# Attention and two expert layers on one core: the second layer's tiles ordered by token count, without a static remainder tile

## The chip, the cores and the metric

The kernel runs on one core of a Trainium2 chip. The metric is the device time of one execution in microseconds. Matmuls run on TensorE; VectorE, ScalarE and GpSimd (POOL) do the rest, and SyncE (SP) issues most transfers.

## What is computed

The output of a clustered attention gives 1536 rows of 512 numbers. Two layers of eight experts follow. In the first, rows with a positive skip score go through the expert of their largest logit. In the second every row goes through one expert, up to a capacity of 384 rows each:

```python
def _moe2_ref(x, w_gate, w1, w2, capacity):
    logits = x @ w_gate
    expert_idx = np.argmax(logits, axis=1)
    ...                                     # gate_w: softmax probability of that expert
    for i in range(N):                      # the first `capacity` rows of each expert are kept
        e = expert_idx[i]
        if counts[e] < capacity:
            disp[e, counts[e]] = x[i]
    ...
    h = np.maximum(np.einsum('ecd,edf->ecf', disp, w1), 0.0)
    y = np.einsum('ecf,efd->ecd', h, w2)    # D = 512, F = 1024
    ...                                     # out[i] = gate_w[i] * y[expert, position]
```

## The kernel before, in words

Attention is followed by `Moe.run`, in which every engine's order is the order of the code. A tile of tokens is a list of row numbers (`gi`), filled by a gather on POOL (`xg`), transposed on TensorE (`psxT`) and copied out by ScalarE; two products with weights `w1` and `w2` follow (L1 and L2), and an indirect output on POOL writes the rows (`fin2`, with `si` as the addresses and `g` as the gates). All outputs write the same tensor, one after the other.

The second layer has these tiles, in this order: 128 slots for rows of expert 0 that skip the first layer (`SU`, the last of the loop over `n1`), 128 slots for expert 0's other rows (`sS`), 256 slots in two parts of 128 for each of experts 1 to 7, and 128 slots for one remainder tile, whose expert is known only at run time (`rO`, `self.SO`). What is still left goes through a loop at the end (`overflow`) that runs as often as a count of remainder tiles says. The first two tiles multiply in plain fp32. The tiles of 256 split weights and activations into two fp32r halves (`wh`, `wl`; `xh`, `xl`; `hh`, `hl`) and use three matmuls for one: an L1 of 8 groups of 128 rows x 4 x 3 = 96 matmuls of 256 columns, and for each part of 128 slots an L2 of 24 matmuls of 512 columns. The remainder tile has a plain L1 and a split L2. PSUM for L1 comes from two buffers (`pL1`); one holds two groups, which ScalarE (`hh`, relu) and VectorE (`hl`) read.

Weights come in eight pieces of 512 KB for each expert, into two alternating sets of buffers. The halves of piece 0 of the next tile are made after the first pair of groups of a tile, pieces 1 to 4 after its L1, and 5 to 7 after its L2 (`nsplit`: first `wh` on ScalarE, then `wl` on VectorE).

Which row goes to which slot is computed with one-hot matrices. `prefix` counts rows before a row on TensorE, `rank` reads the result, `make_R` builds twelve 128 x 128 one-hot matrices `R` on VectorE, and `spread` multiplies them with the columns to be moved. These steps are Python generators (`route2`, `route2b`, `ovinfo`), and `at(t, k, ...)` says before which matmul step of which tile the next piece of them is recorded. `T` is the tile `sS`, and `n1` the tile `SU`; `T, 4` is the fifth of the eight L1 steps of `sS`.

Of the kernel before, what the change touches and what calls it, by code (L numbers as in the profile page):

```python
# [459 lines left out]
class Moe:  # L460
    def __init__(self, ctx, tc, xa, xb, out, w1a, w2a, w1b, w2b, wg2, ident, landA, J=12):
# [44 lines left out]
        nc.gpsimd.iota(self.thr[2][:, 0, :], pattern=[[128, self.nov]], base=128, channel_multiplier=0,  # L506
                       allow_small_or_imprecise_dtypes=True)
# [11 lines left out]
        self.names = con.tile([128, E], F32, name="names")  # L519
        self.ovi = con.tile([128, 1], F32, name="ovi")  # L520
# [366 lines left out]
    def route2(self):  # L887
        V, sm, E, J = self.nc.vector, self.sm, self.E, self.J
        ohp = self.ohp[2]
        V.tensor_tensor(out=ohp, in0=self.acco, in1=self.cm, op=ALU.subtract)  # L890
        T = self.totals(ohp, J, "b", sm)
        yield
        ps = self.prefix(ohp, T, J)
        r = self.r[2]
        self.rank(ohp, ps, J, "b", sm, r)
# [7 lines left out]
        Mf = M.rearrange("p j e s -> p j (e s)")  # L903
        rhs = sm.tile([128, J, 2 * E, 2], BF16, name="rhs2", bufs=1)
        V.tensor_tensor(out=rhs, in0=Mf.unsqueeze(3).to_broadcast([128, J, 2 * E, 2]),
                        in1=self.cols2.unsqueeze(2).to_broadcast([128, J, 2 * E, 2]), op=ALU.mult)
        R = sm.tile([128, J, 128], BF16, name="R", bufs=1)
        self.make_R(R, rp, 0, J)
        yield
        p1 = self.spread(R, rhs, J)  # L910
        inf, t, S = self.ids(p1, 2 * E, sm, "f")
        self.S2 = S
        self.T2 = T
        self.st2 = (R, Mf, inf, t)
        yield

    def route2b(self, cap):
        V, sm, E, J = self.nc.vector, self.sm, self.E, self.J
        R, Mf, inf, t = self.st2
        S = self.S2  # L920
# [4 lines left out]
        self.dests(inf, t, 2 * E, S, sm, "f")  # L925
# [8 lines left out]
        rhs = sm.tile([128, J, 2 * E, 3], BF16, name="rhs5", bufs=1)  # L934
        V.tensor_tensor(out=rhs, in0=Mf.unsqueeze(3).to_broadcast([128, J, 2 * E, 3]),
                        in1=g3.unsqueeze(2).to_broadcast([128, J, 2 * E, 3]), op=ALU.mult)
        yield
        p2 = self.spread(R, rhs, J)
        self.rest(p2, 2 * E, S, sm, "f", 3)
# [119 lines left out]
    def l2(self, hh, hl, W2, rng, ps, sub=0):  # L1059
        nc = self.nc  # L1060
        cs = slice(sub * 128, sub * 128 + 128)
# [33 lines left out]
    def fin2(self, s, ps):  # L1095
        nc, sm = self.nc, self.sm
        y = sm.tile([128, self.D], F32, tag="xy", name="y2")
        nc.scalar.activation(out=y, in_=ps, func=AF.Copy, scale=s["g"])  # L1098
        nc.gpsimd.indirect_dma_start(out=self.out, out_offset=bass.IndirectOffsetOnAxis(ap=s["si"], axis=0),  # L1099
                                     in_=y, in_offset=None, bounds_check=N_TOK - 1, oob_is_err=False)  # L1100
# [131 lines left out]
    def dyn_cum(self, m, idx):  # L1232
# [7 lines left out]
        if m == 1:  # L1240
            V.scalar_tensor_tensor(out=e, in0=self.tix[:, 0:E], scalar=es, in1=self.names, op0=ALU.is_equal, op1=ALU.mult)
            V.tensor_reduce(out=es, in_=e, axis=AX.X, op=ALU.add)
# [53 lines left out]
    def run(self, lg, cap):  # L1296
        nc, E = self.nc, self.E
        n1 = E + 2
        N = n1 + E + 1
# [4 lines left out]
        def load(n, i, t=None):  # L1304
            if n >= N:
                return
            if n == N - 1:
                w = self.load(2, self.rO, n, i, t)
            elif n < n1:
# [3 lines left out]
            else:  # L1313
                w = self.load(2, n - n1, n, i, t)
# [5 lines left out]
        rL = {}  # L1320
# [23 lines left out]
        r1, r1c, r2, r2b = self.route1(lg), self.route1c(), self.route2(), self.route2b(cap)  # L1344
        W2 = lambda t: [L[t, i] for i in range(4, 8)]
        X = {}
        sub = lambda t: [self.S2[2 * t], self.S2[2 * t + 1]]
        PS = {}

        def alloc_x(t):  # L1350
            X[t] = [self.big.tile([128, 4, 256], F32R, name=n) for n in ("xh", "xl")]

        def xts(t, i):
# [4 lines left out]
            sl = slice(i * 128, i * 128 + 128)  # L1358
# [3 lines left out]
        def l1(t, k, hh, hl):  # L1362
            ps = self.pL1.tile([128, 2, 256], F32, tag="l1", name="psl1")
            xh, xl = X[t]
            for q in range(2):
                f = 2 * k + q
                for c in range(4):
                    wh, wl = SP[n1 + t, c]
                    fs = slice(f * 128, f * 128 + 128)
                    nc.tensor.matmul(ps[:, q, :], wh[:, fs], xh[:, c, :], start=(c == 0), stop=False)  # L1370
                    nc.tensor.matmul(ps[:, q, :], wh[:, fs], xl[:, c, :], start=False, stop=False)  # L1371
                    nc.tensor.matmul(ps[:, q, :], wl[:, fs], xh[:, c, :], start=False, stop=(c == 3))  # L1372
            sl = slice(2 * k, 2 * k + 2)
            nc.scalar.activation(out=hh[:, sl, :], in_=ps, func=AF.Relu)
            nc.vector.scalar_tensor_tensor(out=hl[:, sl, :], in0=ps, scalar=0.0, in1=hh.bitcast(F32)[:, sl, :],  # L1375
                                           op0=ALU.max, op1=ALU.subtract)

# [9 lines left out]
        def put2():  # L1387
            self.gather(2, self.S2[0])
# [48 lines left out]
        at(n1, 10, nx(r2), put2, nx(r2b))  # L1437
# [20 lines left out]
        sS = self.S2[0]  # L1458
# [6 lines left out]
        at(T, 0, nx(r2b))  # L1465
        at(T, 3, nx(r2b))
# [9 lines left out]
        ov = self.ovinfo(2)  # L1476
        self.count(2, self.T2)
        eO = self.dyn_cum(2, 0)
        for t in range(1, E + 1):
            n = n1 + t  # L1480

            def nsplit(*ii):
                for i in ii:
                    if n + 1 < N and (t + 1 < E or i >= 4):
                        split(n + 1, i)

            if t == E - 2:
                self.rO = self.reg(eO)
            if n + 2 < N:
                for i in range(4, 8):  # L1490
                    load(n + 2, i)
            hh, hl = self.new_h(256)
            if t < E:
                nxt = sub(t + 1) if t + 1 < E else self.SO[0:1]
                for s in nxt:
                    self.gather(2, s)
                for k in range(4):
                    l1(t, k, hh, hl)
                    if k == 0:
                        nsplit(0)  # L1500
            else:
                nxt = []
                for k in range(2):
                    self.l1_native(self.SO[0]["xt"], [L[n, i] for i in range(4)], k, hh[:, :, 0:128], hl[:, :, 0:128])
# [5 lines left out]
            for i, s in enumerate(sub(t) if t < E else self.SO[0:1]):  # L1510
                ps = self.ps2()
                W2 = [SP[n, j] for j in range(4, 8)]
                self.l2(hh, hl, W2, range(0, 4), ps, i)
                if i == 1 and t + 1 < E:
                    xts(t + 1, 1)
                self.l2(hh, hl, W2, range(4, 8), ps, i)
                self.fin2(s, ps)
                if i == 0 and t + 1 < E:
                    xts(t + 1, 0)
                elif t < E and i == 0:  # L1520
                    self.xt_native(self.SO[0])
            nsplit(5, 6, 7)
        self.overflow(2, [L[N - 1, i] for i in range(8)], 1)
# [92 lines left out]
```

## Time and profile before

| | |
|---|---|
| median of three runs | 669.7 us (669.12 to 671.2) |
| the profiled execution's own time | 668.53 us |
| its span on the core | 666.7 us |
| TensorE busy | 634.2 us, 95% |
| VectorE, ScalarE, GpSimd busy | 63%, 57%, 40% |
| HBM traffic over the span | 152 GB/s |

The span is what the profile shows of the core, from its first to its last instruction; the time holds about 2 us more. Matmuls are pipelined, so the busy time of one is longer than its pace.

### The profile page before, as it was taken

To read this page: it belongs to the slowest core of one execution; us is meant where nothing else is said; L and a number is where in the kernel's file an instruction comes from. 1 tells how busy PE (TensorE), PEld (TensorE's weight loads), DVE (VectorE), ACT (ScalarE), POOL (GpSimd) and SP (SyncE) were. 2 spreads that over 40 slices of the span, in tenths; PEclk is the share of its full clock that TensorE was granted. 3 is DMA by queue.
4 is the path that set the end of the run, shared out by engine and by line. 5 is a ranking of instruction groups with operands and counts; after the bars stand their busy time and mean duration, and the time that the engine had idled before them with its cause. 6 is when DMAs were issued, how large, how long until landed. Compare 5 with 4: busy or idle time off the path is not lost. (4 is left out here: it accounts for less than half of the span.)

```text
span 666.7 us, 11852 instructions
## 1 busy us (share of the span) xinstructions
PE 634.2 (95%) x4238; PEld 547.3 (82%) x4238; DVE 418.1 (63%) x1027; ACT 379.9 (57%) x626; POOL 263.4 (40%) x194
## 2 busy tenths in 40 slices
PE   7889999999998999999999999999999999999994
PEld 6768888888877788887798888986799889888984
DVE  5958666666778774334967766636854955646421
ACT  5767787878777779851443444312544546446340
POOL 7666676767666688800211111101022312302210
PEclk8999999999999999999999999999999999999998
DMA  8964838484834469421677888861596477367100
GB/s 234 210 129 116 204 82 202 82 195 92 205 65 92 119 165 371 124 80 52 186 279 277 313 314 314 328 242 48 187 374 233 166 262 257 129 230 260 36 32 3
DMA packets 78960, 121.49 MB, mean 182 GB/s; under 512 B 27569, under 2 KB 42929, under 8 KB 78896
## 3 DMA queue, kind: packets, MB, share of 16 engines
q1 hardware_dynamic: 74416, 108.18, 53.4%
q0 software_dynamic: 4480, 12.50, 5.7%
q8 instruction: 35, 0.57, 0.4%
q14 instruction: 29, 0.24, 0.1%
HBM read 87.90 MB, written 13.37 MB: 152 GB/s over the span
## 5 line engine op out<-in xcount | busy, mean ns | idle before, releaser
L301 POOL TENSOR_TENSOR Pl<-P,Ph 128x768 fp32r<-128x768 f32 x93 | 170.4, 1841 | 67.7 <-ACT Ph L299 33.4
L983 DVE TENSOR_TENSOR wl<-l,wh 128x1024 fp32r<-128x1024 f32 x92 | 109.2, 1220 | 51.5 <-ACT wh L982 51.0
L272 DVE TENSOR_REDUCE m<-psx 128x1 f32<-128x384 f32 x192 | 97.9, 549 | 33.3 <-PE psx L271 32.1
L290 PE MATMUL pss<-BB,AA 128*128 128x384 f32 (+1 forms) x384 | 88.2, 352 | 9.4 <-DVE lg L372 3.6
L298 ACT ACTIVATE P<-pss 128x384 f32<-128x384 f32 x192 | 84.0, 489 | 21.8 <-PE pss L290 17.0
L982 ACT CAST wh<-l 128x1024 fp32r<-128x1024 f32 x92 | 92.5, 1048 | 0.0
L299 ACT CAST Ph<-P 128x768 fp32r<-128x768 f32 x96 | 80.1, 835 | 4.3 <-PE pso L318 1.2
L290 PEld LDWEIGHTS pss<-BB,AA 128*128 128x128 f32 (+1 forms) x384 | 65.5, 190 | 16.0 <-ACT P L298 4.1
L1005 PE MATMUL psl<-xt,l 128*128 128x128 f32 x640 | 78.0, 277 | 0.4 <-ACT xt L1153 0.4
L1005 PEld LDWEIGHTS psl<-xt,l 128*128 128x128 f32 x640 | 74.9, 192 | 1.7 <-ACT xt L1153 0.5
L1099 POOL DMA_INDIRECT out_dram<-y,fsi x15 | 15.8, 1055 | 130.8 <-ACT y L1098 123.4
L316 PE MATMUL pso<-Ph,VA 128*65 128x384 f32 x192 | 65.5, 341 | 0.7 <-ACT DN L333 0.7
L318 PE MATMUL pso<-Ph,VL 128*64 128x384 f32 x192 | 65.7, 342 | 0.0
L320 PE MATMUL pso<-Pl,VA 128*65 128x384 f32 x192 | 65.3, 340 | 0.2 <-DVE Pl L301 0.2
L1370 PE MATMUL psl<-xh,wh 128*128 128x256 f32 x224 | 62.5, 279 | 2.5 <-DVE hl L1375 2.5
L1371 PE MATMUL psl<-xl,wh 128*128 128x256 f32 x224 | 62.0, 277 | 0.7 <-DVE xl L1360 0.7
L1372 PE MATMUL psl<-xh,wl 128*128 128x256 f32 x224 | 61.9, 276 | 0.0
L271 PE MATMUL psx<-AA,BB 128*128 128x384 f32 x192 | 51.6, 352 | 3.8 <-DVE m L272 1.4
L1091 POOL DMA_INDIRECT xb<-x,fsi x8 | 8.1, 1014 | 102.6 <-DVE x L1090 88.1
L1065 PE MATMUL psl<-wh,hh 128*128 128x512 f32 x120 | 48.2, 402 | 0.0
L1067 PE MATMUL psl<-wl,hh 128*128 128x512 f32 x120 | 47.2, 393 | 0.0
L1066 PE MATMUL psl<-wh,hl 128*128 128x512 f32 x120 | 46.8, 390 | 0.0
(403 smaller groups left out, 1186.9 us busy)
## 6 DMA issues: line engine op xcount, KB each, us to landing
l<-in_moe_w_dram SPq DMA_DIRECT2D x136, 512.0 KB, 7.1
AA<-qkH SPq DMA_DIRECT2D x14, 384.0 KB, 4.8
vn<-in_v_dram SPq DMA_DIRECT2D x8, 384.0 KB, 4.9
BB<-qkL SPq DMA_DIRECT2D x16, 192.0 KB, 3.1
xa<-xn SPq DMA_DIRECT2D x8, 384.0 KB, 3.1
xb<-xn SPq DMA_DIRECT2D x8, 384.0 KB, 4.1
AA<-qkL SPq DMA_DIRECT2D x31, 96.0 KB, 3.8
BB<-qkH SPq DMA_DIRECT2D x31, 96.0 KB, 3.0
```

Source lines behind the costliest of these rows:

```text
L272: nc.vector.tensor_reduce(out=hs[h]["m2"][:, qc, f:f + 1], in_=ps, axis=AX.X, op=ALU.max)
L290: nc.tensor.matmul(ps, AA[0:K, t, kc * 128:(kc + 1) * 128], BB[0:K, t, sl], start=(t == 0), stop=(t == 1))
L298: nc.scalar.activation(out=P[:, f * HF:(f + 1) * HF], in_=ps, func=AF.Exp, scale=1.0 / 8.0)
L299: nc.scalar.copy(Ph, P)
L301: eng.tensor_tensor(out=Pl, in0=P, in1=Ph.bitcast(F32), op=ALU.subtract)
L316: nc.tensor.matmul(o[0:D + 1, :], va, Ph[:, sl], start=(kc == 0), stop=False)
L318: nc.tensor.matmul(o[0:D, :], vl, Ph[:, sl], start=False, stop=False)
L320: nc.tensor.matmul(o[0:D + 1, :], va, Pl[:, sl], start=False, stop=(kc == C - 1))
L982: nc.scalar.copy(h, src)
L983: nc.vector.tensor_tensor(out=l, in0=src, in1=h.bitcast(F32), op=ALU.subtract)
L1005: nc.tensor.matmul(st[k][:, q, :], L1[c][:, f * 128:(f + 1) * 128], xt[:, c, :], start=(c == 0), stop=(c == 3))
L1370: nc.tensor.matmul(ps[:, q, :], wh[:, fs], xh[:, c, :], start=(c == 0), stop=False)
```

## The change

Experts 2 to 7 of the second layer are sorted by their counts at run time (`sort2`), and place `p` of the order, not expert `p`, owns a tile. The tiles have fixed sizes, `caps` = 128, 256, 320, 256, 256, 256, 256, 128; places 0 and 1 stay with experts 0 and 1. Weight addresses of places 2 to 7 are read from `namei2` into a register. A tile of 320 has three parts (128, 128, 64), one PSUM group at a time, and a piece of `h` of its own (`h3`). The remainder tile and its `ovinfo` step are gone from the straight part of the program, and the loop now starts at the first remainder tile. The routing is made in two rounds: `route2` finds the slots of experts 0 and 1, `sort2` those of the sorted order.

```diff
+        self.caps = [128, 256, 320] + [256] * (E - 4) + [128]
+        self.slots = [(p, i) for i in range(3) for p in range(E) if self.caps[p] > 128 * i]
...
+        self.kb = iota([128, E], [[-1, E]], E, 0, "kb")
+        for dst, base in [(self.thr[2][:, p, :], w) for p, w in enumerate(self.caps) if w != self.c0[2]] + \
+                [(self.kb[:, 0:1], 2 ** 18), (self.kb[:, 1:2], 2 ** 17)]:
+            nc.gpsimd.iota(dst, pattern=[[128, dst.shape[1]]], base=base, channel_multiplier=0,
+                           allow_small_or_imprecise_dtypes=True)
...
     def route2(self):
...
-        M = sm.tile([128, J, E, 2], BF16, name="M2", bufs=1)
-        V.tensor_tensor(out=M[:, :, :, 1], in0=ohp, in1=self.bc(s, E), op=ALU.mult)
-        V.tensor_tensor(out=M[:, :, :, 0], in0=ohp, in1=M[:, :, :, 1], op=ALU.subtract)
...
+        cnt = self.ps()[:, 0:E]
+        for b in range(2):
+            self.nc.tensor.matmul(cnt, self.ones, T[:, b], start=(b == 0), stop=(b == 1))
...
+        V.scalar_tensor_tensor(out=self.key2, in0=cnt, scalar=16.0, in1=self.kb, op0=ALU.mult, op1=ALU.add)
...
+    def sort2(self):
...
+        V.tensor_tensor(out=c, in0=key.unsqueeze(1).to_broadcast(G), in1=key.unsqueeze(2).to_broadcast(G), op=ALU.is_ge)
+        V.tensor_reduce(out=pos, in_=c, axis=AX.X, op=ALU.add)
+        V.tensor_tensor(out=c, in0=pos.unsqueeze(1).to_broadcast(G), in1=one.unsqueeze(2).to_broadcast(G), op=ALU.is_equal)
+        V.tensor_tensor(out=c, in0=c, in1=self.tix[:, 0:E].unsqueeze(1).to_broadcast(G), op=ALU.mult)
+        V.tensor_reduce(out=self.names2, in_=c, axis=AX.X, op=ALU.add)
+        V.tensor_copy(self.namei2, self.names2)
+        V.tensor_tensor(out=tv, in0=self.ohx, in1=pos.unsqueeze(1).to_broadcast([128, J, E]), op=ALU.mult)
+        V.tensor_reduce(out=pv, in_=tv, axis=AX.X, op=ALU.add)
+        ohp = self.ohp[2]
+        V.tensor_tensor(out=ohp, in0=self.bc(pv, E), in1=one.unsqueeze(1).to_broadcast([128, J, E]), op=ALU.is_equal)
+        yield
...
+        V.tensor_tensor(out=rhs, in0=M.unsqueeze(3).to_broadcast([128, J, K, 2]),
+                        in1=self.cols2.unsqueeze(2).to_broadcast([128, J, K, 2]), op=ALU.mult)
+        yield
+        inf, t, S = self.ids(self.spread(self.R2, rhs, J), K, sm, "v")
...
+        self.T2 = self.totals(ohp, J, "v", sm)
         yield
...
     def run(self, lg, cap):
...
-        N = n1 + E + 1
+        N = n1 + E
...
+            if n >= n1:
+                p = n - n1
+                if p > 1 and p not in r2n:
+                    r2n[p] = self.reg(self.namei2[:, p:p + 1])
+                w = self.load(2, r2n.get(p, p), n, i, t)
...
         def l1(t, k, hh, hl):
-            ps = self.pL1.tile([128, 2, 256], F32, tag="l1", name="psl1")
...
+            W = self.caps[t]
+            Q = 2 if W <= 256 else 1
+            for f0 in range(2 * k, 2 * k + 2, Q):
+                ps = self.pL1.tile([128, Q, W], F32, tag="l1", name="psl1")
...
+                for (h, l), a, b in [((hh, hl), 0, min(W, 256))] + ([(self.h3, 256, W)] if W > 256 else []):
+                    nc.scalar.activation(out=h[:, sl, 0:b - a], in_=ps[:, :, a:b], func=AF.Relu)
+                    nc.vector.scalar_tensor_tensor(out=l[:, sl, 0:b - a], in0=ps[:, :, a:b], scalar=0.0,
+                                                   in1=h.bitcast(F32)[:, sl, 0:b - a], op0=ALU.max, op1=ALU.subtract)
...
-        at(n1, 10, nx(r2), put2, nx(r2b))
+        at(n1, 10, nx(r2), put2, nx(rs))
+        at(n1, 13, nx(rs))
+        at(n1, 14, nx(r2b))
...
-        at(T, 0, nx(r2b))
-        at(T, 3, nx(r2b))
+        at(T, 0, nx(rs))
+        at(T, 1, nx(r2b))
+        at(T, 4, nx(r2b))
...
-        ov = self.ovinfo(2)
         self.count(2, self.T2)
-        eO = self.dyn_cum(2, 0)
-        for t in range(1, E + 1):
+        Z = E - 1
+        for t in range(1, E):
...
-            if 2 <= t <= 4:
-                next(ov)
...
-        self.overflow(2, [L[N - 1, i] for i in range(8)], 1)
+        self.overflow(2, [L[N - 1, i] for i in range(8)])
```

The first place where rows move is VectorE where the first layer hands over to the second. Before, the slots of all experts come in one round; `finf`, `ft` and `fgi` are the row numbers read from PSUM, `Ff`, `pT` and `urk` belong to the true ranks, `fsi` are output addresses:

```order
L648 COPY finf<-psq 128x32
L649 SCALAR_TENSOR_TENSOR ft<-finf 128x16
L650 TENSOR_SCALAR fgi<-ft 128x16
L923 CAST Ff<-acco 128x96
L604 TENSOR_REDUCE pT<-Ff 128x16
L657 TENSOR_SCALAR fz<-finf 128x16
L658 SCALAR_TENSOR_TENSOR fsi<-ft,fz 128x16
L1143 TENSOR_TENSOR accg<-accg,psq 128x36
L625 TENSOR_TENSOR urk<-Ff,psq 128x96
```

In the changed kernel the same place holds the sort and the masks of the sorted order (`ohx` is the one-hot matrix by expert, `ohp` the one by place), before the true ranks begin:

```order
L660 TENSOR_SCALAR fgi<-ft 128x4
L941 TENSOR_TENSOR rktt<-key_138 128x64
L942 TENSOR_REDUCE skp<-rktt 128x8
L943 TENSOR_TENSOR rktt<-skp,tix 128x64
L944 TENSOR_TENSOR rktt<-rktt,tix 128x64
L945 TENSOR_REDUCE names_136<-rktt 128x8
L946 CAST namei_137<-names_136 128x8
L947 TENSOR_TENSOR uval<-ohx,skp 128x96
L948 TENSOR_REDUCE skv<-uval 128x12
L950 TENSOR_TENSOR ohp_126<-skv,tix 128x96
...
L961 TENSOR_TENSOR rhs_6267<-M_6263,cols_119 128x360
```

Nine operations of the sort, three masks and a product stand between `fgi` and `Ff`; `urk` comes another six rows later.

The second place is VectorE at the start of the second tile of the loop (expert 2 before, place 2 after). Before, the last three weight halves (`wl`) of the tile ahead are followed by one `hl` of 512 columns for each pair of groups:

```order
L1360 TENSOR_TENSOR xl<-psxT,xh 128x4x128 x2
L983 TENSOR_TENSOR wl<-l_1_6441,wh 128x1024
L983 TENSOR_TENSOR wl<-l_2_6443,wh 128x1024
L983 TENSOR_TENSOR wl<-l_3_6445,wh 128x1024
L1375 SCALAR_TENSOR_TENSOR hl<-psl_6731,hh 128x512
L983 TENSOR_TENSOR wl<-l_0_6617,wh 128x1024
L1375 SCALAR_TENSOR_TENSOR hl<-psl_6762,hh 128x512
```

After, the three halves stand at the same place, and two pieces follow for each single group, the second of them into `hA` (the piece `h3`):

```order
L1420 TENSOR_TENSOR xl<-psxT,xh 128x4x64
L1037 TENSOR_TENSOR wl<-l_1_6509,wh 128x1024
L1037 TENSOR_TENSOR wl<-l_2_6511,wh 128x1024
L1037 TENSOR_TENSOR wl<-l_3_6513,wh 128x1024
L1438 SCALAR_TENSOR_TENSOR hl<-psl_6824,hh 128x256
L1438 SCALAR_TENSOR_TENSOR hA<-psl_6824,hA 128x64
L1438 SCALAR_TENSOR_TENSOR hl<-psl_6841,hh 128x256
L1438 SCALAR_TENSOR_TENSOR hA<-psl_6841,hA 128x64
L1037 TENSOR_TENSOR wl<-l_0_6692,wh 128x1024
```

One buffer of PSUM is free after two rows where one row freed it before, and holds half as many groups.

## Rows read from the trace of the kernel before

**Rows 1.** Busy time in stretches of the second layer: stretch, length, engines, PEclk, DMA share.

```profile
core 0: us, PE busy (x) PEld busy (x) DVE busy (x) ACT busy (x) POOL busy (x), PEclk, DMA share, GB/s
480.76:491.73 10.97, 10.97 (x100) 10.97 (x98) 5.87 (x15) 3.42 (x5) 3.19 (x3) 1.00 1.04 393
491.73:497.22 5.49, 5.49 (x27) 4.46 (x25) 4.41 (x5) 4.38 (x5) 0.00 (x0) 1.00 1.03 400
497.22:497.57 0.35, 0.35 (x5) 0.35 (x4) 0.35 (x1) 0.15 (x1) 0.00 (x0) 1.00 0.97 386
503.62:515.23 11.61, 11.17 (x97) 10.96 (x96) 6.52 (x7) 6.16 (x8) 4.47 (x3) 1.00 0.63 217
562.48:563.14 0.66, 0.66 (x27) 0.66 (x25) 0.00 (x0) 0.46 (x1) 0.00 (x0) 1.00 1.01 394
598.90:622.40 23.50, 23.06 (x154) 20.78 (x153) 13.22 (x14) 12.29 (x16) 5.15 (x4) 1.00 0.54 196
645.44:658.27 12.83, 12.82 (x89) 11.46 (x87) 4.79 (x5) 4.71 (x6) 0.99 (x1) 1.00 0.06 22
```

**Rows 2.** Timeline of TensorE, waits in brackets: start, us, instruction.

```profile
509.69 0.38 PE L1370 MATMUL psl<-xh,wh 128*128 128x256 f32 x1 [0.44 <-DVE hl L1375]
...
528.09 0.39 PE L1371 MATMUL psl<-xl,wh 128*128 128x256 f32 x1 [0.70 <-DVE xl L1360]
```

**Rows 3.** DMA page of the stretch with the last output alone, 658 to 663.

```profile
DMA packets 80, 0.02 MB, mean 4 GB/s; under 512 B 75, under 2 KB 75, under 8 KB 80
```

**Rows 4.** Costliest groups of the whole span: busy, mean ns of one.

```profile
L290 PE MATMUL pss<-BB,AA 128*128 128x384 f32 (+1 forms) x384 | 88.2, 352 | 9.4 <-DVE lg L372 3.6
...
L318 PE MATMUL pso<-Ph,VL 128*64 128x384 f32 x192 | 65.7, 342 | 0.0
```

**Rows 5.** Timeline of VectorE in the loop's second tile.

```profile
505.53 3.50 DVE L983 TENSOR_TENSOR wl<-l,wh 128x1024 fp32r<-128x1024 f32 x3 [3.17 <-ACT wh L982]
508.94 0.68 DVE L1375 SCALAR_TENSOR_TENSOR hl<-psl,hh 128x512 fp32r<-128x512 f32 x1
...
524.80 2.04 DVE L630 TENSOR_SCALAR R<-iob,oslF 128x128 bf16<-128x128 bf16 x12
```

**Rows 6.** Busy time in two stretches, early and after the last matmul.

```profile
12.61:16.02 3.41, 3.09 (x16) 2.31 (x17) 1.85 (x5) 2.80 (x4) 2.12 (x5) 0.50 1.02 224
...
661.00:661.50 0.50, 0.00 (x0) 0.00 (x0) 0.00 (x0) 0.00 (x0) 0.00 (x0) 0.64 0.06 17
```

**Rows 7.** Timeline of TensorE in the native tile sS.

```profile
464.09 0.19 PE L615 MATMUL psq<-pT,U 128*128 128x48 bf16 x1
...
464.99 2.94 PE L1005 MATMUL psl<-xt,l 128*128 128x128 f32 x24 [0.42 <-ACT xt L1153]
...
472.17 0.45 PE L640 MATMUL psq<-rhsU,R 128*128 128x3 bf16 x12
...
473.84 7.03 PE L1071 MATMUL psl<-l,hh 128*128 128x512 f32 x16
```

**Rows 8.** Timeline of VectorE at the handover.

```profile
453.81 0.25 DVE L626 TENSOR_REDUCE r<-brk 128x12 f32<-128x96 f32 x1
...
459.32 0.17 DVE L650 TENSOR_SCALAR fgi<-ft 128x16 int32<-128x16 f32 x1
...
469.16 2.03 DVE L630 TENSOR_SCALAR R<-iob,rU 128x128 bf16<-128x128 bf16 x12
```

**Rows 9.** Timelines of POOL: its first DMA, an output and a gather.

```profile
9.13 0.86 POOL L250 DMA_DIRECT2D AA<-qkH  x1 [1.66 <-DVE qkH L159]
...
475.32 1.02 POOL L1099 DMA_INDIRECT out_dram<-y,csi  x1 [11.37 <-ACT y L1098]
...
485.01 1.03 POOL L950 DMA_INDIRECT xg<-xb,fgi  x1 [0.30 <-issue]
```

**Rows 10.** DMA issues of the whole span: KB each, median us to landing.

```profile
l<-in_moe_w_dram SPq DMA_DIRECT2D x136, 512.0 KB, 7.1
...
xg<-xb,fgi POOLq DMA_INDIRECT x15, 5.1
...
out_dram<-y,csi POOLq DMA_INDIRECT x1, 7.6
```

More of the change, by code (lines that the diff above doesn't have):

```diff
@@ L909, in route2 @@
         yield
[L910 to L914, printed above, removed]
+        inf, t, S = self.ids(self.spread(R, rhs, J), 4, sm, "f")
+        self.S2 = {(0, 0): S[0], (1, 0): S[2], (1, 1): S[3]}
+        self.R2 = R
+        yield
+    def sort2(self):
+        V, sm, E, J = self.nc.vector, self.sm, self.E, self.J
+        G = [128, E, E]
+        one = self.tix[:, 1:E + 1]
+        c = sm.tile(G, F32, name="rktt", bufs=1)
+        pos = sm.tile([128, E], F32, name="skp", bufs=1)
+        pv = sm.tile([128, J], F32, name="skv", bufs=1)
+        tv = sm.tile([128, J, E], F32, name="uval", bufs=1)
+        key = self.key2
+        V.tensor_tensor(out=c, in0=key.unsqueeze(1).to_broadcast(G), in1=key.unsqueeze(2).to_broadcast(G), op=ALU.is_ge)
[9 more added lines that the diff above has]
+        yield
+        K, o = len(self.slots), 0
+        M = sm.tile([128, J, K], BF16, name="M2", bufs=1)
+        for i in range(3):
+            ps = [p for p, j in self.slots if j == i]
+            n = len(ps)
+            V.tensor_tensor(out=M[:, :, o:o + n], in0=ohp[:, :, ps[0]:ps[0] + n], in1=self.bc(self.smk[:, :, i], n), op=ALU.mult)
+            o += n
+        self.M2 = M
+        rhs = sm.tile([128, J, K, 2], BF16, name="rhs2", bufs=1)
+        V.tensor_tensor(out=rhs, in0=M.unsqueeze(3).to_broadcast([128, J, K, 2]),
+                        in1=self.cols2.unsqueeze(2).to_broadcast([128, J, K, 2]), op=ALU.mult)
+        yield
+        inf, t, S = self.ids(self.spread(self.R2, rhs, J), K, sm, "v")
+        for k, d in self.S2.items():
+            S[self.slots.index(k)] = d
+        self.dests(inf, t, K, S, sm, "v")
+        self.S2 = dict(zip(self.slots, S))
+        self.P2 = S
+        self.T2 = self.totals(ohp, J, "v", sm)
@@ L933, in route2b @@
         V.tensor_copy(self.cols5[:, :, 2:5], g3)
-        rhs = sm.tile([128, J, 2 * E, 3], BF16, name="rhs5", bufs=1)
-        V.tensor_tensor(out=rhs, in0=Mf.unsqueeze(3).to_broadcast([128, J, 2 * E, 3]),
-                        in1=g3.unsqueeze(2).to_broadcast([128, J, 2 * E, 3]), op=ALU.mult)
+        K = len(self.slots)
+        rhs = sm.tile([128, J, K, 3], BF16, name="rhs5", bufs=1)
+        V.tensor_tensor(out=rhs, in0=self.M2.unsqueeze(3).to_broadcast([128, J, K, 3]),
+                        in1=g3.unsqueeze(2).to_broadcast([128, J, K, 3]), op=ALU.mult)
         yield
-        p2 = self.spread(R, rhs, J)
-        self.rest(p2, 2 * E, S, sm, "f", 3)
+        p2 = self.spread(self.R2, rhs, J)
+        self.rest(p2, K, self.P2, sm, "v", 3)
         rhsU = sm.tile([128, J, 3], BF16, name="rhsU3", bufs=1)
@@ L1457, in run @@
         psU = ps
-        sS = self.S2[0]
+        sS = self.S2[0, 0]
         self.xt_native(sS)
@@ L1475, in run @@
         self.fin2(sS, psS)
-        ov = self.ovinfo(2)
         self.count(2, self.T2)
-        eO = self.dyn_cum(2, 0)
-        for t in range(1, E + 1):
+        Z = E - 1
+        for t in range(1, E):
             n = n1 + t
+            for i in range(4, 8):
+                load(n + 2, i)
             def nsplit(*ii):
                 for i in ii:
-                    if n + 1 < N and (t + 1 < E or i >= 4):
+                    if t + 1 < Z or t + 1 == Z and i >= 4:
                         split(n + 1, i)
[L1487 to L1491, printed above, removed]
-            hh, hl = self.new_h(256)
[L1493 to L1497, printed above, removed]
-                    l1(t, k, hh, hl)
[L1499 to L1504, printed above, removed]
@@ new lines, in run @@
+            hh, hl = self.new_h(256)
+            if self.caps[t] > 256:
+                h3 = self.rt.tile([128, 2, 8, 64], F32R, name="hA")
+                self.h3 = h3[:, 0], h3[:, 1]
+            nxt = sub(t + 1) if t < Z else []
+            for s in nxt:
+                self.gather(2, s)
+            for k in range(4 if t < Z else 2):
+                if t < Z:
+                    l1(t, k, hh, hl)
+                else:
+                    self.l1_native(sub(t)[0]["xt"], [L[n, i] for i in range(4)], k, hh[:, :, 0:128], hl[:, :, 0:128])
+                if k == 0:
+                    nsplit(0)
@@ L1505, in run @@
             nsplit(1, 2, 3, 4)
-            if 2 <= t <= 4:
-                next(ov)
             for i in range(4):
                 load(n + 2, i)
-            for i, s in enumerate(sub(t) if t < E else self.SO[0:1]):
+            pre = [lambda i=i: xts(t + 1, i) for i in range(len(nxt))] if t + 1 < Z else \
+                [lambda: self.xt_native(nxt[0])] if nxt else []
+            for i, s in enumerate(sub(t)):
                 ps = self.ps2()
+                w = width(t, i)
                 W2 = [SP[n, j] for j in range(4, 8)]
[L1513 to L1521, printed above, removed]
+                self.l2(hh, hl, W2, range(0, 4), ps, i, w)
+                if pre and (i or len(pre) == 3):
+                    pre.pop(0)()
+                self.l2(hh, hl, W2, range(4, 8), ps, i, w)
+                self.fin2(s, ps, w)
+                if pre and i == 0:
+                    pre.pop(0)()
```

95 lines of the change are left out of this document (49 added, 46 removed).

## Prediction

> **What bounds the kernel now.** I read the second layer tile by tile, first in the windows of single stages, then in the waits of TensorE, then in the other engines' timelines at the places where TensorE waits.
>
> In [rows 1] the reader is to see that from 480.76 us on TensorE is the bound and little else. The first product of expert 1's tile fills 10.97 us of 10.97, one second product of 128 slots 5.49 of 5.49, a whole later 256-slot tile is 23.06 busy of 23.50, and the remainder tile 12.82 of 12.83, all at a granted clock of 1.00 (2.4 GHz). VectorE (13.22) and ScalarE (12.29) have half of the 23.50 free, and the DMA engines are at 0.54. So a tile costs its matmuls times their pace: 10.97 / 96 = 114 ns for 256 columns, 5.49 / 24 = 229 ns for 512. The little that TensorE waits is in [rows 2]: 0.44 us at the third PSUM pair of the second tile, until VectorE has written `hl`, and 0.70 in the third tile, until VectorE has written `xl`.
>
> How full the slots are is not in the diff, but in the inputs. The reference on its drawn inputs gives experts 0 to 7 counts of 164, 147, 248, 244, 125, 186, 156 and 266, and the native tile of 128 takes 81 of expert 0's first. Hence only expert 7 passes 256, by ten tokens. The trace agrees: the remainder tile's output moved 0.02 MB [rows 3], ten rows of 2 KB.
>
> **The tiles.** In the new order the lists are 83, 147, 266, 248, 244, 186, 156, 125, and they fit 128, 256, 320, 256, 256, 256, 256, 128 with nothing left over, so the loop for the remainder has no pass. The last static tile has the form of the old remainder tile (native first product, split second) and costs the same 12.83. What goes is one 256-slot tile: -23.50 [rows 1].
>
> **The tile of 320.** Its first product is still 96 matmuls, now of 320 columns. Between 114 and 229 ns that is 114.3 + 64/256 x 114.5 = 143 ns: 13.72 us, +2.75. Its third part holds 64 slots, but takes 24 matmuls of 512 columns like a full one. Whether half a stationary operand is cheaper, [rows 4] tell: 64 columns by 384 take 342 ns, 128 columns by 384 take 352. So +5.49; the bound below, were time to follow the slots, is 2.75. The third part's transposes add 0.35 [rows 1].
>
> **A wait that grows.** The 320-wide PSUM tile holds one 128-row group instead of two, so each of the two buffers lasts 1.72 us of matmuls instead of 2.74. At the second tile's start (503.62) VectorE still has three weight splits from the tile before: they start at 505.53, when ScalarE gives the first half, and `hl` is begun at 508.94 [rows 5]. The order of the change keeps those splits ahead of the first `hl`. TensorE runs dry after two groups, 3.43 us after the start. The first group's buffer comes free after two `hl` pieces (256 and 64 columns; from 0.68 for 512 I estimate 0.35 and 0.2) plus 0.07, at 5.9 us. So it stands idle 2.47 us where it lost 11.61 - 10.97 = 0.64 before: +1.83. Bounds: 0 if the splits come earlier, 3.2 if VectorE takes as long for each piece as for 512 columns. Later groups need about 1.1 us of evacuation per 1.72 us of matmuls and don't wait.
>
> In that idle stretch the clock matters. After the last matmul of the kernel, at 658.27, the granted clock is still at full level until about 661 [rows 6], 2.7 us later, so a gap of 2.47 should pass at 2.4 GHz, with little to spare. The Trainium skill (TensorE: Matmul & The Clock Gate, section "Why this matters for your kernels") advises against idle gaps between bursts of matmuls, since the clock returns to its lower level; by that rule this stretch, not the tile count, would be the place to look. The trace has no such gap in the second layer; rival 2 prices it.
>
> **What the static remainder cost elsewhere.** Its slot numbers were computed on VectorE in tiles 2 to 4 and spread on TensorE in 0.66 us [rows 1]; the first part, whose last step runs from 524.80 to 526.84 on VectorE [rows 5], made `xl` late by 0.70 [rows 2]. Both go: -1.36.
>
> **The handover to the second layer.** The route is now made in two rounds: first for experts 0 and 1, then the sort, then all slots. Row by row: VectorE gets five more small operations before `R`, drops one mask, and saves as much again with masks of 48 and 96 columns instead of 96 and 384. The sort's nine operations follow `fgi` (459.32) at about 0.25 to 0.3 each (the reduce of 96 columns is 0.25 [rows 8]): 2.5 us, then masks and their product, 1.4: ready at about 463.5, before TensorE gets there at 464.09 [rows 7]. So the second spread finds its operand, and its 0.3 us lies in the time up to 464.99 in which TensorE waits for `xt`. The true-rank prefix, which lay in that time, comes one step of 0.93 later and costs about 0.45 on the path (464.09 to 464.99 less the 0.42 of waiting). With it the operand `rhs5` and all that VectorE does behind it move by about 1.9 us; `R` for the native tile, done at 471.19 [rows 8], ends at 473.1, and TensorE, which wants it at 472.17 + 0.45 [rows 7], waits 0.5. Together +0.9; bounds 0.4 (the wait is absorbed) and 2.4 (the whole shift appears).
>
> Behind that, the output of the native tile slips by 2 us. On POOL it starts at 475.32 and lands 7.6 later [rows 9, 10]; the next output, which writes the same tensor, waits for that, and the gathers behind it start at 485.01. They would start at 487 and land by 494.6 even at those 7.6; the first one is needed after expert 1's first product and half a second one, at 480.76 + 0.9 + 10.97 + 2.75 = 495.4. Nothing is added, but the margin is under a microsecond.
>
> **At nothing.** Weight addresses come from registers: tile 2's name is ready near 461, and its first load waits for a buffer that TensorE frees at 473.84 [rows 7]. Five more IOTAs at the start run in the 1.66 us in which POOL waits before its first DMA [rows 9]; uncovered they would cost well under 1. A ninth expert's weights are no longer loaded, 4 MB in a stage that doesn't wait for DMA.
>
> **Sum.** -23.50 + 2.75 + 5.49 + 0.35 + 1.83 - 1.36 + 0.90 = -13.54. From the profiled execution's 668.53 that is 655.0. The median of the three runs is 669.7, 1.2 above it, which gives 656.2. I take the middle, 655.6.
>
> **The rivals.**
> 1. No new stall in the 320 tile: VectorE gets its `hl` in early. For it: VectorE is half idle there. Against: the order puts the splits first. -1.83 and the old 0.64 gone: 653.1.
> 2. The gap lowers TensorE's clock. For it: the margin of [rows 6] is small. The stretch at 1.2 GHz that the trace has, early in attention, is 3.41 us long [rows 6]; at half pace that loses 1.7: 657.3.
> 3. The handover costs its upper bound, or the first gather is late: +1.5 to +2, 657.3.
> 4. The other side: a list is too long and the loop for the remainder makes a pass. It decides when the shortest list passes 128 (it has 125), the longest 320 (266) or the next 256 (248). A pass is in series: 12.83 for the products, 4 MB of weights at about 395 GB/s [rows 1] 10.6, a gather of 5.1 [rows 10], 28.5 together even without its output: 684, slower by 14. The counts speak against it, and the ten rows of [rows 3] bear them out.
> 5. The change doesn't give what it says, since loads by register come late: each late weight tile costs up to its 7.1 us [rows 10]. One such wait leaves -6.4: 662.7. Against it: the first layer loads by register too.
>
> **How the numbers follow.** The sum has 0.70 (654 to 657 by its small bounds), rival 1 0.07, rivals 2 and 3 0.08 each, rival 5 0.04, rival 4 0.03. The time is that of the sum. The range goes from rival 1 to rivals 2 and 3 with half a microsecond on the slow side: 653.0 to 658.3. A measurement of this kernel can tell about 0.3%, 2 us; all cases but rival 4 are faster by more: 0.96, with 0.01 for no difference and 0.03 for slower.
>
> **What would show it.** Right: the second tile lasts about 33.6 us instead of 23.50, with one wait near 2.5 us at its third group, on `hA` or `hl`; no matmul of the output `ogi`; five tiles of 256 in place of seven, each near 23.5; TensorE ends near 644.7 at clock 1.00. The spread of 30 columns starts without a wait. Wrong: a wait for `xg` in expert 1's tile, a wait for weights `l`, PEclk under 1.00 after the gap, or a pass of the loop behind the last tile.

## The result, and the profile after

The changed kernel takes 659.83 us in the median of six runs (658.66 to 660.74); the kernel before took 670.11 beside it. The ratio is 0.9845, with a 95% interval of 0.983 to 0.986. The gain is 10.3 us where 14 were predicted, and the time lies 1.5 us above the predicted range.

The profiled execution took 660.25 us with a span of 658.4, so 8.3 less than the span before, where the sum said 13.54. Stretches of the changed kernel, in the columns of [rows 1]; the first is in attention, the second the first product of expert 1's tile, then the first product of the 320 tile, the whole 320 tile, the piece of it at the lower clock, a 256 tile, and the last tile:

```profile
212.80:216.21 3.41, 3.41 (x14) 3.05 (x13) 2.52 (x6) 0.90 (x2) 1.82 (x1) 0.50 0.01 2
483.37:494.76 11.39, 11.39 (x99) 11.39 (x98) 6.43 (x12) 3.55 (x6) 4.33 (x4) 1.00 1.05 389
507.17:525.62 18.45, 15.73 (x97) 15.47 (x96) 9.19 (x18) 8.49 (x19) 4.46 (x3) 0.91 0.63 230
507.17:543.06 35.89, 33.17 (x177) 28.50 (x176) 15.85 (x26) 15.32 (x29) 6.53 (x5) 0.95 0.40 148
513.18:516.59 3.41, 3.02 (x11) 3.05 (x12) 2.10 (x4) 1.42 (x3) 0.28 (x1) 0.50 0.98 345
543.06:566.55 23.49, 23.06 (x153) 20.79 (x152) 13.23 (x14) 12.27 (x16) 5.48 (x4) 1.00 0.59 214
636.99:649.81 12.82, 12.82 (x89) 11.46 (x87) 4.79 (x5) 4.71 (x6) 0.99 (x1) 1.00 0.02 6
```

The 320 tile is the dear one: 35.89 us, where 33.6 was predicted, and its rows are the only ones of the second layer with a clock under 1.00. TensorE's wait in it, in its timeline:

```profile
513.57 0.61 PE L1432 MATMUL psl<-xh,wh 128*128 128x320 f32 x1 [2.72 <-DVE hA L1438]
```

VectorE in the same place, to be held against [rows 5]: three weight halves, then two pieces for each group:

```profile
509.08 3.50 DVE L1037 TENSOR_TENSOR wl<-l,wh 128x1024 fp32r<-128x1024 f32 x3 [3.64 <-ACT wh L1036]
512.49 0.42 DVE L1438 SCALAR_TENSOR_TENSOR hl<-psl,hh 128x256 fp32r<-128x256 f32 x1
513.20 0.23 DVE L1438 SCALAR_TENSOR_TENSOR hA<-psl,hA 128x64 fp32r<-128x64 f32 x1 [0.29 <-ACT hA L1437]
```

Between `hl` and `hA` VectorE waits 0.29 us for ScalarE, and ScalarE's timeline says why: its relu into `hA` begins only when `hl` is done.

```profile
512.94 0.22 ACT L1437 ACTIVATE hA<-psl 128x64 fp32r<-128x64 f32 x1 [1.72 <-DVE hl L1438]
```

So the prediction's wait is there, at its place and on its tile, and the clock fell to 1.2 GHz before TensorE went on. By the two spans the 5.2 us between the sum and the trace are: 1.80 in attention, which the change doesn't touch; 0.59 in expert 1's tile (23.80, for 22.86 before and 0.35 of transposes); 2.79 in places 2 to 6, of which 2.32 in the 320 tile; 0.10 behind the last matmul; and 0.1 less in the handover (483.37 for 480.76, less the 1.80, is 0.81; predicted 0.90).

### The profile page after: what moved, and what is told of

Its sections match the earlier page's. It is cut to its first block, busy times and chain, and to the rows that moved or that the text cites. A ratio compares the mean times of both kernels' runs of the same rounds, so it can differ in the third digit from the quotient of the medians.

```text
span 658.4 us, 11633 instructions
## 1 busy us (share of the span) xinstructions
PE 623.5 (95%) x4104; PEld 536.0 (81%) x4104; DVE 404.0 (61%) x1003; ACT 370.6 (56%) x624; POOL 259.7 (39%) x197
## 5 line engine op out<-in xcount | busy, mean ns | idle before, releaser
L1037 DVE TENSOR_TENSOR wl<-l,wh 128x1024 fp32r<-128x1024 f32 x84 | 99.9, 1221 | 57.1 <-ACT wh L1036 57.1
L1036 ACT CAST wh<-l 128x1024 fp32r<-128x1024 f32 x84 | 84.4, 1045 | 0.0
L1156 POOL DMA_INDIRECT out_dram<-y,vsi x15 | 15.1, 1005 | 134.5 <-ACT y L1155 115.3
L1432 PE MATMUL psl<-xh,wh 128*128 128x256 f32 (+1 forms) x192 | 55.7, 290 | 4.5 <-DVE hA L1438 2.7
L1433 PE MATMUL psl<-xl,wh 128*128 128x256 f32 (+1 forms) x192 | 54.9, 286 | 0.0
L1434 PE MATMUL psl<-xh,wl 128*128 128x256 f32 (+1 forms) x192 | 54.8, 285 | 0.0
L271 PEld LDWEIGHTS psx<-AA,BB 128*128 128x128 f32 x192 | 34.1, 189 | 11.3 <-ACT P L298 5.0
L1122 PE MATMUL psl<-wh,hh 128*128 128x512 f32 x104 | 41.9, 403 | 0.0
L1432 PEld LDWEIGHTS psl<-xh,wh 128*128 128x128 f32 x192 | 36.6, 191 | 5.8 <-issue 3.0
```

Source lines behind the costliest of these rows:

```text
L271: nc.tensor.matmul(ps, BB[:, 0, qc * 128:(qc + 1) * 128], AA[:, 0, f * HF:(f + 1) * HF], start=True, stop=True)
L1036: nc.scalar.copy(h, src)
L1037: nc.vector.tensor_tensor(out=l, in0=src, in1=h.bitcast(F32), op=ALU.subtract)
L1432: nc.tensor.matmul(ps[:, q, :], wh[:, fs], xh[:, c, 0:W], start=(c == 0), stop=False)
```

## The experiments

**The same kernel again.** Nothing is edited.

> The changed kernel once more, with nothing edited. Its profiled execution was 660.25 us, its median 659.83. Two things in its trace are to be seen again or not: the granted clock of 0.50 at 513.18 to 516.59 us, right after the wait of 2.72 us at the third group of the 320-slot tile, and the one at 212.80 to 216.21 us in attention, in code that the change doesn't touch. Theory 1 (the wait lowers the clock, the attention drop is chance): the first comes again at the same distance from the wait, the second needn't; 658.4 to 660.5. Rival (both drops come and go with the execution, whatever the waits are): the first is missing in some executions, and one without both takes about 3 us less, 657.3. Also looked at: whether the first-layer matmuls of expert 1's tile take 118 ns each again (114 before the change).

> The changed kernel a third time, unedited. So far one profiled execution had a granted clock of 0.50 for 3.41 us right behind the wait of 2.72 us at the third group of the 320-slot tile, and one with a wait of 2.71 us had none. Theory 2 (the wait makes room for the drop, but whether it comes hangs on the execution): either can be seen; with it the tile takes near 35.9 us, without it near 34.8. The attention drop near 212 us may come or not, and is worth 1.5 us.

`same` took 658.57 us (four runs, 656.79 to 659.75; ratio to before 0.9834, 0.981 to 0.9859), and its trace has neither fall of the clock. The first product of its 320 tile and the whole tile:

```profile
505.63:522.95 17.32, 14.58 (x98) 14.10 (x96) 9.10 (x18) 8.51 (x19) 4.47 (x3) 1.00 0.66 245
505.63:540.38 34.75, 32.01 (x177) 27.12 (x176) 15.76 (x26) 15.34 (x29) 6.54 (x5) 1.00 0.43 153
```

```profile
512.03 0.38 PE L1432 MATMUL psl<-xh,wh 128*128 128x320 f32 x1 [2.71 <-DVE hA L1438]
```

The wait is the same, 2.71 us, and the product takes 17.32 instead of 18.45: the lower clock costs 1.13 us, not the 1.7 of rival 2. Of its 3.41 us 0.39 lie in the wait; in the rest a matmul of 320 columns starts every 267 ns, which is less than twice 147; and the slower start spares a second, short stall that `same` has at the fifth group. No bracket marks that stall, but 0.33 us lie between two starts there, where 0.15 is the pace:

```profile
515.48 0.30 PE L1434 MATMUL psl<-xh,wl 128*128 128x320 f32 x1
515.81 0.38 PE L1432 MATMUL psl<-xh,wh 128*128 128x320 f32 x1
516.03 0.31 PE L1433 MATMUL psl<-xl,wh 128*128 128x320 f32 x1
```

`same2`, one execution of 661.18 us, had the fall again, and 18.34:

```profile
513.71:517.12 3.41, 2.83 (x11) 2.86 (x12) 2.10 (x4) 1.61 (x4) 0.48 (x1) 0.50 0.91 312
```

So an equal wait brings the lower clock in some executions only. Theory 1 of the first expectation, in which the fall surely follows the wait, is wrong, and its rival's 657.3 for an execution without either fall is near the 657.71 of the profiled one.

**The wait taken away.** The splits of pieces 5 to 7 are moved from ahead of a tile's first product into it, with the loads that reuse their buffers; in places 2 to 6 (`own_all`), or in place 2 alone (`own_2`).

```diff
+            own = [5, 6, 7] if t in [2, 3, 4, 5, 6] else []
             for i in range(4, 8):
-                load(n + 2, i)
+                if i not in own:
+                    load(n + 2, i)
...
-                if k == 0:
+                if k < len(own):
+                    split(n, own[k])
+                    load(n + 2, own[k])
+                if k == len(own):
                     nsplit(0)
```

> In each of the tiles 2 to 6, the splits of the last three pieces of its weights (pieces 5 to 7, 1.05 us of ScalarE and 1.22 us of VectorE each) move from ahead of its first layer to behind its first, second and third pair of blocks, and the loads that reuse their landing buffers move with them. All else stays. Theory 1 (the wait for a buffer of the third group is made by the three splits ahead of it, and lowers the clock): the wait of 2.72 us, 0.50 clock (about 1.45 us) and four waits of 0.43 us go, together 5.9, so 654.0 (653 to 655.5). Rival A (the clock drop is not tied to the wait): 4.4 less, 655.4, with a 0.50 stretch still in that tile. Rival B (the splits now stand between the relus, and a relu waits for a split of 1.22 us on VectorE in each group): the waits come back as 0.3 to 1 us in three groups of each tile, and the time stays within 2 us of 659.8.

> The same move of three splits in the 320-slot tile alone. Theory 1: the 2.72 us wait and the 0.50 stretch behind it go, 4.2 less than the changed kernel: 655.7. If only the wait goes and the clock drops all the same (rival A): 657.1. The four waits of 0.43 us in the 256-slot tiles stay. If other work takes the place of the wait in that tile (rival B): 658 to 660.

`own_all` took 651.92 us (650.98 to 654.09; ratio 0.9734, 0.9714 to 0.9754), `own_2` 656.85 (655.96 to 659.62; ratio 0.9803, 0.9784 to 0.9822). Neither trace has a fall of the clock in the second layer ahead of the last matmul. First product of the 320 tile and one 256 tile of `own_all`:

```profile
507.51:522.89 15.38, 14.56 (x97) 14.08 (x96) 7.69 (x16) 7.32 (x17) 3.07 (x3) 1.00 0.34 106
...
540.29:563.08 22.79, 22.79 (x154) 20.71 (x152) 13.51 (x14) 12.38 (x16) 4.70 (x4) 1.00 0.65 219
```

The 256 tile has TensorE busy for all of its 22.79 us, where a tile took 23.50 before [rows 1]: the short wait at the third pair costs not its 0.44 but 0.71. Around it the starts of three matmuls lie 0.72 and 0.22 us apart, where two paces are 0.23, since the bracket begins only at the modelled end of the matmul ahead, and the one behind a wait takes 0.38 us [rows 2]. In the two traces places 2 to 6 take 6.3 us less than in the changed kernel, where 5.9 were expected. The median fell further, to 651.92 for the 654.0 expected; the profiled execution, with 654.09, is the slowest of the five, and what the quicker ones lack is not shown. `own_2` lies 1.1 us above the 655.7 of its theory 1; its trace has no fall in the tile, but keeps a wait of 0.80. Rival B is right in a small way: a wait of 0.79 us is left, at the fifth group of the 320 tile and not, as the expectation of the next run says, at the third.

> All five tiles split pieces 5 to 7 within their own first layer, as in the run of 651.9 us, and in the 320-slot tile both relus of a group (256 and 64 columns) stand on ScalarE ahead of both differences on VectorE. In the runs so far the relu into hA waited 0.49 us in every group until VectorE had written hl, and own_all kept a wait of 0.79 us at the third group, until VectorE had written hA. Theory 1 (the wait is the order of these four, hh, hl, hA, hA): the wait of 0.79 falls by about 0.4 or goes, 651.2. Rival (the wait is the split or the y of the tile ahead that stands before the first relu on ScalarE): 0.79 stays, and the time is 651.9.

```diff
-                for (h, l), a, b in [((hh, hl), 0, min(W, 256))] + ([(self.h3, 256, W)] if W > 256 else []):
+                parts = [((hh, hl), 0, min(W, 256))] + ([(self.h3, 256, W)] if W > 256 else [])
+                for (h, l), a, b in parts:
                     nc.scalar.activation(out=h[:, sl, 0:b - a], in_=ps[:, :, a:b], func=AF.Relu)
+                for (h, l), a, b in parts:
```

With both relus ahead of both differences the 0.79 is gone too, and the profile marks no wait of TensorE from 478 us to its last matmul. 651.41 us (650.93 to 652.87, six runs; ratio 0.9709, 0.9682 to 0.9735): the fastest version, 8.4 us under the changed kernel, though not told apart from `own_all`. Its first product of 320 columns, and its whole 320 tile, without any wait:

```profile
507.50:521.65 14.15, 14.15 (x98) 14.09 (x96) 7.30 (x17) 6.99 (x18) 3.08 (x3) 1.00 0.37 115
507.50:539.08 31.58, 31.58 (x177) 27.12 (x176) 14.91 (x26) 14.65 (x29) 5.68 (x5) 1.00 0.50 168
```

That gives the real price of the columns: 14.15 / 96 = 147.4 ns, not 143.

**The wait made shorter and longer.** `own_2_last` moves one split of the three in place 2, `chain` only the order of the four readers, `gap_long` puts a fourth split ahead (`nsplit(0)` before the loop over `k` for place 2); `gap_long2` is the same kernel once more. Each was executed once.

```diff
+            own = [7] if t in [2] else []                  # own_2_last, else as own_all
```

```diff
+            if t == 2:                                     # gap_long
+                nsplit(0)
             for k in range(4 if t < Z else 2):
...
-                if k == 0:
+                if k == 0 and t != 2:
                     nsplit(0)
```

> In the 320-slot tile alone, only the split of piece 7 moves from ahead of the first layer to behind its first pair of groups. Two splits stay ahead, so the wait at the third group falls by one split, 1.2 us, from 2.71 to about 1.5. Theory 2: no clock of 0.50 in that tile, which takes 34.8 - 1.2 = 33.6 us. Rival (no tie): the drop can come there as before, then 34.7.

> Only the order of the four readers of a group in the 320-slot tile changes: both relus on ScalarE first, then both differences on VectorE. In the changed kernel the relu into hA begins when VectorE's hl ends, and VectorE then waits 0.29 us for it. Theory 1 (the prediction's wait of 2.47 us was exceeded because of that handshake): VectorE frees the first buffer 0.28 earlier, and the wait at the third group falls from 2.71 to 2.43 us. Rival (it was exceeded because the splits start later than before): the wait stays at 2.7. A clock of 0.50 behind the wait may come or not.

> In the 320-slot tile alone, piece 0 of the next tile's weights is split ahead of the first group instead of behind the first pair, so that four splits, not three, stand ahead of the first hl on VectorE. The wait at the third group grows by one split, 1.2 us, to 3.9. Theory 2 (longer waits make the drop more likely): the 0.50 clock follows the wait, and the tile takes 34.8 + 1.2 + 1.1 = 37.1 us. Rival (drops come and go by themselves, with no tie to the wait): no drop there, or one elsewhere; the tile takes 36.0.

> The kernel with four splits ahead of the first hl of the 320-slot tile once more. Its wait of 3.85 us was followed by 6.83 us at a granted clock of 0.50. Theory 2 (the longer the wait, the surer the drop): a drop again, with its start inside the wait, some 2 us or more after the last matmul ahead of it. Rival (by chance): none.

| run | the execution, us | wait at the third group, us | clock 0.50 in that tile, us | first product, us |
|---|---|---|---|---|
| `own_2_last` | 657.22 | 1.58, and 0.56 later | none | 16.94 |
| `chain` | 658.68 | 2.34 | 511.43 to 514.84 | 18.03 |
| `same` | 657.71 | 2.71 | none | 17.32 |
| `same2` | 661.18 | 2.72 | 513.71 to 517.12 | 18.34 |
| the changed kernel | 660.25 | 2.72 | 513.18 to 516.59 | 18.45 |
| `gap_long` | 660.93 | 3.85 | 511.87 to 518.69 | 20.60 |
| `gap_long2` | 660.81 | 3.85 | 515.72 to 519.13 | 19.74 |

The two rows of `gap_long`, one from the timeline of TensorE, one from its windows:

```profile
513.39 0.61 PE L1432 MATMUL psl<-xh,wh 128*128 128x320 f32 x1 [3.85 <-DVE hA L1438]
```

```profile
511.87:518.69 6.82, 5.30 (x20) 5.33 (x21) 2.38 (x7) 1.33 (x5) 0.28 (x1) 0.50 0.98 348
```

The wait of `own_2_last`, that of `chain` and its fall, and the fall of `gap_long2`:

```profile
511.25 0.39 PE L1432 MATMUL psl<-xh,wh 128*128 128x320 f32 x1 [1.58 <-DVE hA L1438]
...
511.78 0.60 PE L1432 MATMUL psl<-xh,wh 128*128 128x320 f32 x1 [2.34 <-DVE hA L1440]
511.43:514.84 3.41, 3.06 (x11) 3.10 (x12) 1.79 (x5) 0.00 (x0) 0.63 (x1) 0.50 1.01 343
...
515.72:519.13 3.41, 3.41 (x15) 3.41 (x15) 0.65 (x2) 0.61 (x2) 0.00 (x0) 0.50 1.04 391
```

The matmul behind the wait shows the state at a glance: 0.61 us where the clock has fallen, 0.38 where it is full. With no wait over 1.6 us the tile shows no fall (`own_2_last`, `own_2`, `own_all`, `own_all_chain`), nor does any tile of the second layer in the four traces of the kernel before, where no wait is over 0.71; with 2.3 to 2.7 it shows one in three executions of four; with 3.85 in two of two. The falls begin 2.0 to 2.3 us after TensorE's last matmul ahead of the wait, in `gap_long2` 5.3, when it had been running again for 1.4. That the falls come by themselves, with no tie to the wait, is hard to hold against this. The whole 320 tile took 38.00 and 37.18 us in `gap_long` and `gap_long2`, where the first expectation has 37.1 with a fall and 36.0 without; in `own_2_last` it took 34.38 for 33.6, since a second wait of 0.56 came up.

`chain` also settles the size of the wait. VectorE frees the first buffer 3.96 us after its first split starts instead of 4.35, and the wait falls by 0.38, to 2.34 for the 2.43 expected, so the handshake between ScalarE and VectorE was what the estimate of 2.47 lacked:

```profile
507.67 3.50 DVE L1037 TENSOR_TENSOR wl<-l,wh 128x1024 fp32r<-128x1024 f32 x3 [3.65 <-ACT wh L1036]
511.08 0.42 DVE L1440 SCALAR_TENSOR_TENSOR hl<-psl,hh 128x256 fp32r<-128x256 f32 x1
511.41 0.22 DVE L1440 SCALAR_TENSOR_TENSOR hA<-psl,hA 128x64 fp32r<-128x64 f32 x1
```

**Other terms.** Two sizes of the large tile, `cap256` in the changed kernel, `cap288` in the fastest version; `cap256` also skips the masks of the third part, which is then empty:

```diff
-        self.caps = [128, 256, 320] + [256] * (E - 4) + [128]
+        self.caps = [128, 256, 256] + [256] * (E - 4) + [128]     # cap288: 288 in the third place
```

> The third place gets 256 slots instead of 320, so that the ten tokens that a third part holds in the changed kernel go through a pass of the remainder loop behind the last tile. This is the prediction's fourth rival, made on purpose. The tile gets shorter by 2.75 to 3.1 (matmul columns), 5.5 (third part), 0.35 (transposes), about 2.3 (wait falls to 0.43) and about 1.45 (clock): 12.5 us; the loop's pass costs at least 28.5 by the prediction's working. So 676 (672 to 682). If a pass cost under 12 us, a third part would have been the dearer way, and the time would be under 660.

It took 690.21 us, dearer than the 672 to 682 expected. From the last matmul of the static tiles (639.9) to the end are 48.6 us, in the changed kernel 8.6, so a pass costs 40, not 28.5. Two rows of TensorE in the loop, and the whole stretch, show what the sum of 28.5 lacked: the gather and then the weights of the second product are each waited for, and the granted clock, at 0.70 in the mean, is 0.50 from 642.59 to 663.07 and for 3.41 us more.

```profile
652.84 1.11 PE L1049 MATMUL psxT<-idw,xg 128*128 128x128 f32 x4 [10.40 <-DMA xg<-xb,poi]
...
670.21 8.64 PE L1130 MATMUL psl<-l,l 128*128 128x512 f32 x16 [3.12 <-DMA l<-in_moe_w_dram]
```

```profile
639.90:688.50 48.60, 22.29 (x109) 15.62 (x108) 6.71 (x37) 3.15 (x5) 3.73 (x3) 0.70 0.30 98
```

The rest is in the static tiles: they end 9.9 us earlier than in the changed kernel, not 12.5, since in this execution 256 columns took 120 ns instead of 113.

> On top of the best version so far (651.4 us, no wait in the second layer): the large tile gets 288 slots instead of 320, so that its third part has 32 instead of 64. By the prediction's terms the first product follows the columns, 114 + 32/64 x (147 - 114) = 130.5 ns x 96 = 12.5 us instead of 14.15, and the third part's 24 matmuls cost 5.5 us however few slots they have: the tile takes 31.6 - 1.6 = 30.0 us. Rival (the third part follows its slots, the bound of 2.75 us for 64): its matmuls would fall below 230 ns, and the tile would take 28.6 us or less.

One execution took 652.05 us, no less than `own_all_chain`, and the tile 30.61, where 30.0 was expected. First product of the 288 tile, its last part and a half, and the first product of the next tile:

```profile
505.87:518.91 13.04, 12.93 (x97) 12.72 (x96) 6.94 (x17) 6.80 (x18) 3.08 (x3) 1.00 0.44 125
528.06:536.48 8.42, 8.42 (x40) 4.96 (x39) 0.69 (x1) 1.28 (x2) 1.00 (x1) 1.00 0.32 115
536.48:547.79 11.31, 11.31 (x98) 11.31 (x96) 5.59 (x6) 5.29 (x7) 2.97 (x3) 1.00 0.46 137
```

36 matmuls of a second product take 8.42 us, 234 ns each, with 32 slots in the last 24 of them as with 64 (8.37 in the changed kernel): the part's price does not follow its slots. The first product fell by 1.1, less than the 1.6 expected, and this execution ran the first products of its 256 tiles some 4% slower at a full clock (11.31 against 10.90). If the 288 columns were slowed alike, 13.04 x 10.90 / 11.31 = 12.57 is an estimate of what they take otherwise, near the 12.5 expected.

**The kernel before, three times more.**

> The kernel before, unedited, profiled a second time. Its one trace shows no fall of the granted clock in attention, while 11 of 12 profiled executions of the changed kernel and its variants have one of 3.41 us between 211 and 219 us, which costs 1.5 us. Theory 3 (it is no part of the change): it is to be seen in most traces of the kernel before too, between 211 and 219 us, and the last block of attention then ends 1.5 us later than in its first trace (287.79 us for the last P). Rival (the change brings it, by what it adds at the start of the program): none here.

> The kernel before a third time. Theory 3: the attention drop in at least one of the two new traces. Rival: in none. Also looked at: whether its matmuls of 256 columns take 118 instead of 113 ns in some tiles at a granted clock of 1.00.

> The kernel before a fourth time, as the two ahead of it: by theory 3 the attention drop comes in two of three or more, by the rival in none.

Two of the three show the fall in attention, from 211.07 and from 213.05 us; the last row of `P` in ScalarE's timeline of attention starts at 288.78, 290.15 and 287.80 us, in the third, as in the first trace, without it. The window of `before_b`:

```profile
211.07:214.49 3.42, 3.42 (x12) 2.85 (x13) 3.35 (x6) 1.61 (x3) 2.49 (x2) 0.50 0.00 0
```

So the fall belongs to the kernel before as well: two of four there, 11 of 12 of the changed kernel and its variants when these runs were made. Whether the change makes it more frequent, these counts can't settle; it comes without the change too. And the times of these three executions, 668.81 to 671.34, show that the 668.53 from which the sum was made was one of the quick ones.

## Why the prediction was wrong

The forecast of 655.6 was 4.2 us too low. Falls of the clock make 2.6 of the 5.2 us between the sum and the trace, 1.13 in the 320 tile and 1.5 in attention; the one execution known to have neither, in `same`, took 657.71. The rest is mostly the size of the terms for the 320 tile and a slower pace of matmuls in some tiles.

- **The tiles.** Right: one 256 tile less, no pass of the loop, the last tile 12.82 for 12.83. The price of a 256 tile holds: 23.49, 23.83, 23.54 and 23.07 in places 3 to 6 for 23.50; in the one of 23.83 the second half of the first product went at 118 ns a matmul instead of 113.
- **The tile of 320.** The third part is right: full price for 64 slots and for 32. The columns were mis-sized: +2.75 became 96 x (147.4 - 114.3) = +3.18, so 0.43 more. The straight line was drawn to a matmul of 512 columns of the other product; from 256 to 320 columns of this product (113.5 to 147.4 ns in `own_all_chain`) a column costs 0.53 ns, where that line has 0.45.
- **A wait that grows.** The mechanism, its place and its cause are right. The size is not: +1.83 became 17.32 - 14.15 - 0.64 = +2.53 without the clock. Of the 0.70, 0.48 is at the third group, where the stall costs 2.95 with the slower start behind it instead of 2.47: VectorE's two pieces, from the start of the first to the end of the second, take 0.94 where the prediction has "0.35 and 0.2", which left out the handshake between the relu into `hA` and `hl`. Most of the rest is the second stall, of 0.26, at the fifth group, where the prediction says that later groups don't wait; behind it the pace is 147 ns again.
- **"A gap of 2.47 should pass at 2.4 GHz."** This is the step that failed, and rival 2 with its 8% happened: in three executions of four with a wait of 2.3 to 2.7 us the clock fell, for 1.13 us. The wait came out longer than 2.47, but `chain` had the fall behind 2.34 too. The step took one observation for a limit: from the last matmul of one trace to the fall, read as 2.7 us, and 2.9 by the mean clock of 0.64 in [rows 6]. The same stretch at the end of the other fifteen traces reads from 1.9 to 4.7 us. The Trainium skill (TensorE: Matmul & The Clock Gate, section "Why this matters for your kernels") advises against idle gaps between bursts of matmuls, which the prediction set aside. The page has longer gaps in mind than the 2.34 us behind which the clock fell here, and the measurement decides; that a gap can cost the clock, the trace agrees.
- **The static remainder.** About right: the three tiles that bore it took 23.75, 24.25 and 23.78 before, 1.28 over three times 23.50; predicted 1.36.
- **The handover.** Right: 0.81 for 0.90, no wait for `xg`, none for weights. The true-rank prefix takes 0.33 of TensorE's time for 0.45, and the spread that follows `R` takes 0.32 longer, for 0.5 of waiting.
- **The base.** 1.8 us of the difference between the two traces is attention: 0.3 in its start, 1.5 the fall of the clock. The sum stood on an execution of before that had none. Going to the middle between it and the median covered 0.6 of that.
- **Expert 1's tile.** Its first product took 11.39 us for 10.97 at a full clock, with no wait. In five of the traces of the changed kernel and its variants it is 11.39, in five others 10.97 or 10.98, so the change alone doesn't set it; in the four of the kernel before it is always 10.97. The cause is open.

Rival 1, no new stall in the 320 tile, is what `own_2` nearly builds: 656.85, 3 us under the changed kernel, and still 3.7 above the rival's 653.1. Rivals 3, 4 and 5 did not happen.

## What to carry to other kernels

A wait on TensorE costs more than its brackets say: the restart, and a chance of a stretch at 1.2 GHz, which was seen in this second layer behind waits of 2.34 to 3.85 us and behind none of 1.58 or less. When a buffer of PSUM gets smaller, look first at what stands ahead of its first reader on VectorE and ScalarE; moving that work, which nobody needed early, between the readers gave back 8 us, nearly as much as the change itself. And before a sum is made from one profiled execution, see how often the clock's fall in it comes back in another.

## What the runs showed of the hardware

- The same program differs by 3.3 us between two executions, mostly through falls of the clock: none in the second layer and attention of `same` (span 656.0), both in `same2` (659.3), which cost about 1.1 and 1.5 us.
- In some executions runs of matmuls go 4% slower at a granted clock of 1.00: 118 instead of 113 ns for 256 columns, over half a first product in the kernel before (11.82 for 11.62 in a tile of `before_c`, both with the short wait) and over whole ones after the change (11.39 for 10.98 in expert 1's tile, without a wait). No row here says what makes it.
